# Gaps between SBUF tiles that set the distance, modulo 256 bytes, between the feed-forward tiles and the weights

## The chip, the cores and the metric

The kernel runs on one core of one Trainium2 chip. The metric is the device time of one execution in microseconds (us). One execution was also profiled; all rows below are of that one.

## What is computed

The reference has two stages. A gated linear attention runs over 4 batches, 8 heads, 768 positions and a head size of 48:

```
state = alpha[t] * state + outer(k[t], v[t])
y[t]  = q[t] @ state
```

Its output, 3072 tokens of width 384, goes through a feed-forward layer with 2048 hidden units:

```
h   = x @ w_in
g   = 0.5 * h * (1 + erf(h / sqrt(2)))
out = g @ w_out
```

Inputs and output are float32, the two weight matrices float64.

## The kernel before

**Feed-forward part.** The tokens are cut into 12 groups g of 256, the hidden units into 8 pieces f of 256. One (g, f) is a step, so there are 96 steps. To keep float32 precision, every operand of a matmul is split into a high and a low part of type float32r, and three products are added: high by high, high by low, low by high. `gemm1` (line 543) makes, for a step, 18 matmuls of 128 x 128 weights by 256 columns: the weights `wih` and `wil` are loaded as the stationary operand, the tile `x` streams through. Its result, the PSUM tile `hp`, is read twice by ScalarE (`gelus`, lines 555 and 556: GELU to the high half `ghi`, then GELU in place), and VectorE makes the low half `glo` from both (`gelu_low`, line 561). `gemm2` (line 582) makes 12 matmuls of 384 columns: here the halves `ghi` (8) and `glo` (4) are loaded as the stationary operand, and the weights `woh` and `wol` stream. So the weights are the loaded side in gemm1 and the streamed side in gemm2.

On TensorE each matmul is a pair, a weight load (PEld) and a matmul (PE). The load of the next pair begins when the matmul of this pair begins, so both read SBUF at the same time: one reads the next stationary operand, the other the streaming one.

**Order.** The attention units, the conversion of the weights (loaded as float64 and split on the chip) and the steps are put in order ahead of time by a planner in the kernel with costs (`COST`) and ranks; it writes out the order of TensorE, VectorE, ScalarE and SyncE by hand. Of the gemms it keeps gemm1 of step n+1 ahead of gemm2 of step n. From about 370 us on, TensorE runs nothing but steps.

**Where the tiles lie.** SBUF addresses are given per partition. Pools are laid side by side, and tiles in a pool in the order of their first use, each rounded up to 32 bytes. The pool `const` comes first and holds all weights; then `work`; then `ffn` with three x tiles, `z` (the rows of x that a DMA spreads), two `ghi` and two `glo`. At the other end of SBUF lies the pool `stage` for the conversion; when it is done, the pool `late` takes its room and holds one further x tile, for the groups 3, 7 and 11. Adding up the sizes gives:

| tiles | bytes each | address of the first | modulo 256 | distance to the weights, modulo 256 |
|---|---|---|---|---|
| wih, wil, woh, wol (32 tiles) | 3072 | 53,536 | 32 | 0 |
| x of groups 0-2, 4-6, 8-10 (3 tiles) | 6144 | 168,544 | 96 | +64 |
| z | 2048 | 186,976 | 96 | +64 |
| ghi, glo (2 each) | 2048 | 189,024 | 96 | +64 |
| late x of groups 3, 7, 11 | 6144 | 223,200 | 224 | +192 |

All these sizes, and the slices that one matmul reads (512, 1024 or 1536 bytes), are whole multiples of 256, so each tile keeps its distance throughout. The three x tiles go round by the order in which they come free; that gives groups 0, 5, 9 the first, 2, 6, 10 the second and 1, 4, 8 the third.

Names and lines that the change touches: `x_tiles` (line 487 on), `x_high`, `gelus`, `gelu_low` and `gelu_rest`, all of which ask a pool for tiles.

## Time and profile before

| | us |
|---|---|
| median of 3 runs (lowest, highest) | 515.25 (514.54, 515.87) |
| the profiled execution | 515.5 |
| its span, first to last instruction | 513.9 |
| PE busy in the span | 500.7 (97%) |
| DVE, ACT, POOL busy | 297.6, 219.6, 40.3 |

A row of a group of instructions has the line, the engine, the operation, the tiles (written <- read), the form and the count. A matmul's duration in the profile is longer than its distance to the next one, since matmuls overlap in the array; where two matmuls follow each other without a break, duration and distance differ by about 163 ns throughout (a duration of 281 ns goes with a distance of 118 ns), so that a duration that is 4 ns longer means a step that is 4 ns longer per matmul. In this kernel's rows both 32-bit types are written f32.

### The profile page before, as it was taken

The page shows a single profiled execution, that of the slowest core. Times are in us where ns is not written, and L with a number is a line of the kernel's source. Part 1 is how long each engine was busy: PE and PEld are TensorE (multiplying, and loading weights), DVE is VectorE, ACT ScalarE, POOL GpSimd, SP SyncE. Part 2 cuts the span into 40 slices and gives each one's busy share as a digit, 9 for nine tenths or more (in the row PEclk, how much of TensorE's full clock was granted, in tenths as well). Part 3 has the DMA queues.
Part 4 walks back from the last instruction along what each step waited for, and adds up shares of the span by engine and source line. Part 5 has one row for each costly group of instructions (what it writes and reads, how often), then busy time and mean ns, then how long its engine had stood idle before and what let it go on. Part 6 is the DMA issues. An engine that isn't in the chain of part 4 may idle for free.

```text
span 513.9 us, 13811 instructions
## 1 busy us (share of the span) xinstructions
PE 500.7 (97%) x5974; PEld 482.2 (94%) x5974; DVE 297.6 (58%) x579; ACT 219.6 (43%) x468; POOL 40.3 (8%) x60
## 2 busy tenths in 40 slices
PE   8898999999999999999999999999999999999995
PEld 8777999999999999999999999999999999999995
DVE  6999999999849966677685365252232211211211
ACT  2677765555444445355453343344332222222221
POOL 4100110100011111121111011010000000000000
PEclk9999999999999999999999999999999999999999
DMA  8967553531033422433231020010010000000001
GB/s 303 348 198 238 210 151 112 186 124 62 1 124 110 140 94 87 159 100 99 104 110 64 0 75 6 1 42 9 1 40 9 0 33 2 32 0 1 32 1 35
DMA packets 15250, 44.20 MB, mean 86 GB/s; under 512 B 2224, under 2 KB 5728, under 8 KB 15184
## 3 DMA queue, kind: packets, MB, share of 16 engines
q1 hardware_dynamic: 13520, 38.44, 22.7%
q0 software_dynamic: 1232, 4.33, 2.2%
q8 instruction: 49, 0.80, 0.7%
q10 hardware_dynamic: 432, 0.49, 0.3%
q14 instruction: 17, 0.14, 0.1%
HBM read 36.18 MB, written 4.72 MB: 80 GB/s over the span
## 4 chain that ended last, share of the span: by engine, by line
PE 94%; ACT 2%; ACTq 1%; issue 1%; DVE 0%; POOL 0%; DVEq 0%; POOLq 0%
PE acc L582 40%; PE hp L543 39%; PE s L308 4%; PE ybank L464 3%; PE ybank L381 3%; PE ybank L403 2%; PE warm L87 2%; ACTq L535 1%; PE spare L986 1%; PE ybank L349 1%; ACT junk L164 1%; PE ybank L521 0%; ACT L555 0%; ACT x L527 0%; ACT hp L556 0%
## 5 line engine op out<-in xcount | busy, mean ns | idle before, releaser
L543 PE MATMUL hp<-x,wih 128*128 128x256 f32 x1152 | 208.6, 281 | 0.0
L543 PEld LDWEIGHTS hp<-x,wih 128*128 128x128 f32 x1152 | 179.3, 188 | 1.8
L543 PE MATMUL hp<-x,wil 128*128 128x256 f32 x576 | 160.9, 279 | 0.0
L555 ACT ACTIVATE ghi<-hp 128x512 fp32r<-128x512 f32 x96 | 57.4, 598 | 212.5 <-PE hp L543 212.4
L561 DVE TENSOR_TENSOR glo<-hp,ghi 128x512 fp32r<-128x512 f32 x92 | 63.0, 685 | 145.4 <-ACT hp L556 145.2
L582 PE MATMUL acc<-woh,ghi 128*128 128x384 f32 x384 | 132.5, 345 | 0.0
L582 PE MATMUL acc<-wol,ghi 128*128 128x384 f32 x384 | 129.2, 336 | 0.0
L543 PEld LDWEIGHTS hp<-x,wil 128*128 128x128 f32 x576 | 108.0, 188 | 0.0
L582 PE MATMUL acc<-woh,glo 128*128 128x384 f32 x384 | 82.6, 336 | 0.0
L582 PEld LDWEIGHTS acc<-woh,ghi 128*128 128x128 f32 x384 | 72.0, 187 | 3.0
L582 PEld LDWEIGHTS acc<-wol,ghi 128*128 128x128 f32 x384 | 72.1, 188 | 0.0
L582 PEld LDWEIGHTS acc<-woh,glo 128*128 128x128 f32 x384 | 68.4, 188 | 0.0
L556 ACT ACTIVATE hp<-hp 128x512 f32<-128x512 f32 x96 | 56.9, 593 | 0.0
L272 DVE TENSOR_TENSOR_SCAN pp<-akq,top 128x256 f32<-128x256 f32 x48 | 31.3, 680 | 23.6 <-POOL qk L282 21.5
L287 DVE TENSOR_TENSOR_SCAN rp<-akq,rp,top 128x255 f32<-128x255 f32 x48 | 35.3, 763 | 0.7
L282 POOL TENSOR_TENSOR qk<-akq,pp 128x512 f32<-128x512 f32 x18 | 23.8, 1324 | 134.5 <-PE ybank L464 75.9
L607 POOL DMA_DIRECT2D out_dram<-part x11 | 8.4, 762 | 263.2 <-DVE part L601 191.9
L512 ACT CAST x<-ybank 64x256 fp32r<-64x256 f32 (+4 forms) x60 | 20.0, 333 | 10.9 <-PE ybank L464 8.4
L308 PE MATMUL s<-qk,akq 48*64 48x112 f32 x768 | 23.9, 261 | 0.5 <-PE ybank L349 0.2
L516 DVE TENSOR_TENSOR x<-ybank,x 64x256 fp32r<-64x256 f32 (+3 forms) x54 | 19.2, 355 | 8.5 <-ACT x L512 7.6
L317 ACT COPY kn<-s 128x384 f32<-128x384 f32 x24 | 11.5, 480 | 26.2 <-PE s L308 19.3
L464 PEld LDWEIGHTS ybank<-qk,states 48*48 48x48 f32 x704 | 14.6, 119 | 7.3 <-issue 2.8
(78 smaller groups left out, 412.2 us busy)
## 6 DMA issues: line engine op xcount, KB each, us to landing
akq<-in_akq_dram SPq DMA_DIRECT2D x22, 768.0 KB, 4.7
st<-in_moe_w_in_dram SPq DMA_DIRECT2D x8, 768.0 KB, 5.1
st<-in_moe_w_out_dram SPq DMA_DIRECT2D x8, 768.0 KB, 4.4
vn<-in_v_dram SPq DMA_DIRECT2D x12, 384.0 KB, 4.0
out_dram<-part POOLq DMA_DIRECT2D x11, 384.0 KB, 3.1
x<-z SPq DMA_DIRECT2D x63, 32.0 KB, 2.3
akq<-in_akq_dram SPq DMA_DIRECT2D x2, 512.0 KB, 6.1
akq<-in_akq_dram SPq DMA_DIRECT2D x2, 256.0 KB
```

The costliest lines, as they stand in the source:

```text
L272: nc.vector.tensor_tensor_scan(pp[:, i], at[:, i], top, MID, ALU.mult, ALU.min)
L282: eng.tensor_tensor(out=qs[:, :, :, :CS], in0=by_chunk(qt), in1=by_chunk(pp), op=ALU.mult)
L287: nc.vector.tensor_tensor_scan(rp[:, i, G - 2 :: -1], at[:, i, G - 1 : 0 : -1], top[:, 1:], rp[:, i, G - 1 :], ALU.mult, ALU.min)
L308: nc.tensor.matmul(d["s"][o, h, e : e + KW], lhsT=d["kt"][r, i, t], rhs=d["qs"][r, i, j], start=True, stop=True)
L464: ins = nc.tensor.matmul(ybank[o, b, t : t + CS], lhsT=states[u][j][r, i], rhs=d["qs"][r, i, j, :CS], start=False, stop=True, skip_group_c ...
L512: nc.scalar.copy(hi, y)
L516: nc.vector.tensor_tensor(out=lo, in0=y, in1=hi.bitcast(F32), op=ALU.subtract)
L543: nc.tensor.matmul(hp[:, j, :], lhsT=a[:, j, i * P : (i + 1) * P], rhs=x[:, i, :], start=(j == 0 and i == 0 and n == 0), stop=(i == NK - 1 ...
L555: nc.scalar.activation(ghi, hp, AF.Gelu)
L556: nc.scalar.activation(hp, hp, AF.Gelu)
L561: nc.vector.tensor_tensor(out=glo, in0=hp, in1=ghi.bitcast(F32), op=ALU.subtract)
L582: nc.tensor.matmul(acc[t], lhsT=a[:, j, t * C : (t + 1) * C], rhs=w[:, j, :], start=(first and j == 0 and k == 0 and w is wo_hi[f]), stop= ...
```

## The change

A helper `gap` asks the pool for a tile that nothing reads or writes; it takes up room and moves what comes after it. The tiles x, ghi and glo get a tag each, so that each has its own place, and gaps are put ahead of some of them. Going through the new order of the pool (gap 128, x0, z, x1, gap 64, ghi0, glo0, ghi1, gap 192, x2, gap 64, glo1) gives x and z at 224 modulo 256, and ghi and glo at 32. The late tile lies at 224 already. Distances to the weights after the change: all x +192, all halves 0. `HOME` writes down which group takes which x tile, the same as before; the halves go in turn, the same as before. No instruction is added, removed or moved to another place in the order.

```diff
--- before.py
+++ after.py
@@ -31,6 +31,8 @@
 LANES = 8
 RATE, ALONE, LATENCY, SMALL, BEGIN = 350e3, 290e3, 2.1, 50e3, 2.2
 MARGIN = 1.5
+HOME = {0: 0, 1: 1, 2: 2, 4: 1, 5: 0, 6: 2, 8: 1, 9: 0, 10: 2, "s": 1}
+X_GAP, Z_GAP, HI_GAP, LO_GAP, LATE_GAP = (128, 0, 192), 0, (64, 0), (0, 64), 0
 COST = dict(
     scan=0.65, back=0.72, keys=0.65, q=1.35, qv=0.62, scores=1.0, kn=0.5, mask=0.62, inside=1.05, chain=1.15, outer=0.85, carry=0.26, last=0.34, last_p=0.15, sums=0.55, scaled=0.45,
     xh=0.6, xl=0.65, spread=0.62, check=0.95, load=0.46, fetch=0.46, u=0.92, c0=0.56, c1=0.9, c2=0.45, c3=0.95, c4=0.92,
@@ -98,6 +100,10 @@
     top = column("top", TOP).to_broadcast([P, G])
     n_checks = NG * NPAIR // 2
     outside = const.tile([P, 2, n_checks], F32, name="outside")
+
+    def gap(pool, nbytes, name):
+        if nbytes:
+            pool.tile([P, nbytes // 4], F32, name=name, bufs=1)
 
     NB = 2
     vbuf = []
@@ -481,8 +487,12 @@
     def x_tiles(g):
         if g != "s" and g % (XB + 1) == XB:
             x = late[0].tile([P, NK, 2, G], F32R, tag="xl", name=f"x{g}")
+            if g == XB:
+                gap(late[0], LATE_GAP, "gap_late")
         else:
-            x = ffn.tile([P, NK, 2, G], F32R, tag="x", bufs=XB, name=f"x{g}")
+            if g in range(XB):
+                gap(ffn, X_GAP[HOME[g]], f"gap_x{g}")
+            x = ffn.tile([P, NK, 2, G], F32R, tag=f"x{HOME[g]}", bufs=1, name=f"x{g}")
         xt[g] = x[:, :, 0], x[:, :, 1]
         return x
 
@@ -507,6 +517,8 @@
         if u == 0:
             cur[g, "x"] = x_tiles(g)
         else:
+            if g == 0:
+                gap(ffn, Z_GAP, "gap_z")
             cur[g, "z"] = ffn.tile([P, 2, G], F32R, tag="z", bufs=1, name=f"z{g}")
         for y, hi, _ in x_parts(g, u):
             nc.scalar.copy(hi, y)
@@ -550,14 +562,23 @@
                     )
         return hp
 
+    halves = {}
+
+    def half_tile(what, gaps, g, f):
+        n = halves.get(what, 0)
+        halves[what] = n + 1
+        if n < 2:
+            gap(ffn, gaps[n], f"gap_{what}{n}")
+        return ffn.tile([P, 2, G], F32R, tag=f"{what}{n % 2}", bufs=1, name=f"{what}_{g}_{f}")
+
     def gelus(g, f, hp):
-        ghi = ffn.tile([P, 2, G], F32R, tag="ghi", name=f"ghi_{g}_{f}")
+        ghi = half_tile("ghi", HI_GAP, g, f)
         nc.scalar.activation(ghi, hp, AF.Gelu)
         nc.scalar.activation(hp, hp, AF.Gelu)
         return ghi
 
     def gelu_low(g, f, hp, ghi):
-        glo = ffn.tile([P, 2, G], F32R, tag="glo", name=f"glo_{g}_{f}")
+        glo = half_tile("glo", LO_GAP, g, f)
         nc.vector.tensor_tensor(out=glo, in0=hp, in1=ghi.bitcast(F32), op=ALU.subtract)
         return glo
 
@@ -565,7 +586,7 @@
         nc.tensor.matmul(hp, lhsT=minus, rhs=ghi, start=False, stop=True, skip_group_check=True)
 
         def out():
-            glo = ffn.tile([P, 2, G], F32R, tag="glo", name=f"glo_{g}_{f}")
+            glo = half_tile("glo", LO_GAP, g, f)
             nc.scalar.copy(glo, hp)
             return glo
```

## Rows read from the trace of the kernel before

**Rows 1.** page, busy time of each engine, and the chain that ended last
```profile
PE 500.7 (97%) x5974; PEld 482.2 (94%) x5974; DVE 297.6 (58%) x579; ACT 219.6 (43%) x468; POOL 40.3 (8%) x60
...
PE acc L582 40%; PE hp L543 39%; PE s L308 4%; PE ybank L464 3%; PE ybank L381 3%; PE ybank L403 2%; PE warm L87 2%; ACTq L535 1%; PE spare L986 1%; PE ybank L349 1%; ACT junk L164 1%; PE ybank L521 0%; ACT L555 0%; ACT x L527 0%; ACT hp L556 0%
```

**Rows 2.** windows: us, busy PE, PEld, DVE, ACT, POOL (x), PEclk, DMA share, GB/s
```profile
40.00:80.00 40.00, 38.53 (x582) 36.07 (x577) 38.90 (x69) 27.35 (x57) 2.82 (x3) 1.00 0.60 206
...
400.00:440.00 40.00, 40.00 (x286) 40.00 (x285) 7.87 (x12) 9.96 (x19) 0.72 (x1) 1.00 0.03 11
```

**Rows 3.** timeline: the GELU and the subtraction that follow one gemm1, ACT and DVE
```profile
449.77 0.60 ACT L555 ACTIVATE ghi<-hp 128x512 fp32r<-128x512 f32 x1 [3.15 <-PE hp L543]
...
450.89 0.69 DVE L561 TENSOR_TENSOR glo<-hp,ghi 128x512 fp32r<-128x512 f32 x1 [3.54 <-ACT hp L556]
```

**Rows 4.** windows of line 543 alone: us, busy PE, PEld (xinstructions), PEclk, DMA share, GB/s
```profile
80.00:159.30 79.30, 38.37 (x306) 37.28 (x304) 1.00 0.28 93
...
206.50:330.50 124.00, 54.77 (x432) 52.74 (x433) 1.00 0.23 72
330.50:369.20 38.70, 18.15 (x144) 17.57 (x145) 1.00 0.06 17
369.20:472.70 103.50, 54.64 (x432) 53.67 (x433) 1.00 0.04 14
```

**Rows 5.** timeline, PE: start, us: steps begin on x10 (first, second), on x11
```profile
439.01 0.39 PE L543 MATMUL hp<-x,wih 128*128 128x256 f32 x2
...
443.22 0.40 PE L543 MATMUL hp<-x,wih 128*128 128x256 f32 x2
...
472.80 0.39 PE L543 MATMUL hp<-x,wih 128*128 128x256 f32 x2
```

**Rows 6.** timeline, PE: start, us: the late tile x11, up to its last step
```profile
474.84 0.33 PE L582 MATMUL acc<-woh,ghi 128*128 128x384 f32 x1
...
476.92 0.40 PE L543 MATMUL hp<-x,wih 128*128 128x256 f32 x2
...
479.04 0.34 PE L582 MATMUL acc<-woh,ghi 128*128 128x384 f32 x1
...
502.15 0.40 PE L543 MATMUL hp<-x,wih 128*128 128x256 f32 x2
```

**Rows 7.** line 543, min/median/max ns: x10; its last; x11 first step; second; last
```profile
L543 PE MATMUL hp<-x,wih x12: 276/279/279, 439.0 to 440.9; 128*128 128x256 f32 x12
...
L543 PE MATMUL hp<-x,wil x1: 277/277/277, 441.0 to 441.0; 128*128 128x256 f32 x1
...
L543 PE MATMUL hp<-x,wih x11: 275/276/276, 472.8 to 474.5; 128*128 128x256 f32 x11
...
L543 PE MATMUL hp<-x,wih x12: 280/281/281, 476.9 to 478.8; 128*128 128x256 f32 x12
...
L543 PE MATMUL hp<-x,wil x1: 285/285/285, 478.9 to 478.9; 128*128 128x256 f32 x1
```

**Rows 8.** line 543 after a break of PE's stream: x3 (late), then x5 twice
```profile
L543 PE MATMUL hp<-x,wih x12: 276/276/383, 176.0 to 177.9; 128*128 128x256 f32 x12
...
L543 PE MATMUL hp<-x,wih x24: 276/276/384, 252.4 to 256.4; 128*128 128x256 f32 x24
...
L543 PE MATMUL hp<-x,wih x11: 278/279/384, 278.0 to 279.9; 128*128 128x256 f32 x11
```

**Rows 9.** line 582, min/median/max ns: x10, two steps in turn; x11
```profile
L582 PE MATMUL acc<-woh,ghi x4: 333/337/339, 441.1 to 442.2; 128*128 128x384 f32 x4
...
L582 PE MATMUL acc<-woh,ghi x3: 338/338/338, 445.7 to 446.4; 128*128 128x384 f32 x3
...
L582 PE MATMUL acc<-woh,ghi x3: 335/335/335, 479.4 to 480.1; 128*128 128x384 f32 x3
```

**Rows 10.** plain f32 matmuls, min/median/max ns: lines 87 and 365
```profile
L87 PE MATMUL warm<-ident x18: 274/275/275, 7.3 to 9.2; 128*128 128x128 f32 x18
...
L365 PE MATMUL ybank<-states,ident x2: 326/326/326, 26.5 to 26.7; 128*128 128x192 f32 x2
```

## The prediction, made before the result was known

> **What bounds the kernel now.** I read the page first: TensorE is busy in 97% of the span, and the chain that ended last runs through gemm2 (40%) and gemm1 (39%) [rows 1]. The reader should see there that only TensorE's own pace can matter. [...] Nothing else is close: the GELU waited 3.15 us for its gemm1, and the low half, begun at 450.89 and 0.69 us long, waited 3.54 us for ScalarE [rows 3]. So each nanosecond that a matmul is farther from the next one is paid in full, 18 times a step in gemm1 and 12 times in gemm2.

> Then the timeline, for the pace. The eight steps of group 10 lie between 439.01 and 472.80 us: 4.224 us a step [rows 5]. The late tile x11 holds the same work at another address: its last six steps begin from 476.92 to 502.15, 4.205 us each [rows 6]. And its first step took 472.80 to 476.92, 4.12 us: gemm1 2.04 us, 113.3 ns a matmul, where the second step's gemm1 (476.92 to 479.04) has 2.12 us, 117.8 ns [rows 5, 6]. The same matmuls thus run at two paces, and the durations mark them: 276 ns in the first step of x11, 281 in the second, 279 on x10 [rows 7]. In gemm2 there are 335 ns on x11, 338 in one step of x10 and a mix of 333 to 339 in the next [rows 9]. [...]

> **The change, part by part.** No instruction, wait or DMA is added or moved; HOME repeats the places that the x tiles take now, the halves go in turn as before, and a gap costs room alone. What changes is the distance between what streams and what is loaded, modulo 256 bytes.

> *gemm1 on the nine +64 groups goes to +192.* That is the late tile's case, so its price has rows. In an unbroken stream x11 mostly has 281 ns, where +64 has 279: no gain. After a break of TensorE's stream it differs: five gemm1 runs on late tiles came after one (first duration 383 ns or more, at 159.5, 176.0, 184.3, 336.0 and 340.9 us), and all five settled at 276 ns. On +64 tiles after 80 us there are eleven such runs, of which two did (at 149.4 and 252.4); the others stay at 279 [one of each, rows 8]. Nine runs with ten steps can change over: 10 x 18 x 4.4 ns (2.12 less 2.04 us, over 18) = 0.8 us.

> *gemm2, streaming weights, halves loaded: from distance 64 to 0.* No row has a whole gemm2 at 0. The nearest is its price on x11, 335 ns, against 338 and the mix on x10: the halves and weights have the same addresses in both, and only what gemm1 left behind differs. I take that, since gemm1 will be as on x11. With gemm1's small loss it is in the step times: 4.224 less 4.205 is 0.019 us. After 80 us, line 543 has 306, 432 and 432 matmuls on +64 tiles, 65 steps, and 3 x 144, 24 steps, on late ones [rows 4]; four of the 65 are the short ones at 149.4 and 252.4 us. 61 x 0.019 = 1.2 us. Bounds: below, the f32 matmuls of line 365, whose 192 columns stream as long as 384 of float32r (line 87's 128 columns have 275 ns, like 256 of gemm1), have 326 ns, 9 less than 335 [rows 9, 10]; above, the one distance that shows a loss. This is the last matmul of gemm1 on x11, which streams x at 224 while halves at 96 load: 285 ns against 281, 4 more [rows 7].

> *The seams.* The last gemm1 matmul of a late step goes from 285 back to 281: some 16 x 4 ns = 0.06 us. On the other tiles it loads halves at distance 0 now (277 ns against 279 [rows 7]) and at 192 after: at most 4 ns x 65 = 0.26 us lost or nothing; I take nothing, as +192 shows the pace of its tile. The seam from gemm2 to gemm1 stays at 0. z and the DMAs into x keep their sizes.

> Sum: 0.8 + 1.2 + 0.06 = 2.1 us off the profiled 515.5 us (span 513.9 and 1.6 around it), which lies 0.25 above the median of the runs; from the median, **513.2 us**. Both gains are off TensorE's path alone, so nothing takes their place: the halves are ready some 3 us early.

> [...]

> **Rivals.**

> *Short pace throughout.* With gemm2 at 0, gemm1 may be entered as in the first step of x11 and stay at 276 ns: 61 steps and the 16 late ones that are long now, 18 x 4.4 ns = 79 ns each, 6.1 us, and gemm2's 0.02 us in 65 steps, 1.3 us: 507.8. For it: 276 held through whole steps at both distances. Against: of the late tiles' steps that follow gemm2 without a break only two got there, and those behind a gemm2 of a +64 tile.

> *No change.* The paces follow from how a run is entered, both occur at +64 and at +192 [rows 7, 8], and the mix stays; or the gaps don't come out where they should. 515.2, give or take 1. [...]

> *Slower: gemm2 at distance 0.* What streams and what is loaded then begin in the same place modulo 256, twelve times a step. If this costs what +128 costs at the seam, 4 ns over the present 337 or so, then 89 steps x 12 x 4 = 4.3 us, less the 0.9 of the breaks and seams: 518.7. It decides from 0.9 us / 1068 = 0.8 ns a matmul on, measured from now: above 338 ns throughout it is slower. Against it: the seams at 0 show no loss today (277 against 279 [rows 7]).

> **How the numbers follow.** A difference under 0.3%, 1.5 us, can't be told from no change by a measurement of this kernel. Forecast, 511.5 to 514.5: 0.34, of which 0.27 beyond 1.5 us and 0.07 within. Short pace (and anything better, down to the bound of rows 10: 9 ns x 1068 = 9.6 us more): 0.23. No change: 0.19. Slower: 0.24. Together faster 0.50, same 0.26, slower 0.24. For 8 in 10 the range leaves out the best part of the short pace and the worst of the slower case: 506 to 519. The forecast's own range is 511.5 to 514.5.

> **What would show it.** Right: gemm1 on x10 at 281 in an unbroken stream and 276 after breaks, gemm2 at 335 on all tiles, steps of 4.205 us, no 285 at the seam. Short pace: 276 in most steps, 4.12 us. Wrong: gemm2 above 338, or below 333 (then distance 0 has a pace of its own), or any wait of TensorE that is not there now.

## The result, and the profile after

| | before | after |
|---|---|---|
| median of 5 runs, us (lowest, highest) | 514.99 (514.54, 515.87) | 509.92 (509.1, 510.61) |
| ratio of the times, 95% interval | | 0.9894 (0.9881 to 0.9907) |
| the profiled execution, its span, us | 515.5, 513.9 | 510.61, 509.0 |

By that ratio the change is faster by 1.06%, about 5.5 us; the two medians differ by 5.1 us, 0.98%, which is within the interval. The prediction said 513.2, in a range of 506 to 519. The forecast's own range was 511.5 to 514.5, and the measured time lies below it.

First the page of the changed kernel, the busy time of each engine. Lines have moved: gemm1 is line 555 now, gemm2 603.

```profile
PE 495.7 (97%) x5974; PEld 477.0 (94%) x5974; DVE 297.3 (58%) x579; ACT 219.6 (43%) x468; POOL 39.1 (8%) x60
```

TensorE's busy time fell by 5.0 us, about as much as the span; DVE and ACT have what they had [rows 1]. Where it went shows in the timeline of TensorE (start, duration; the first row of a step, and one of its gemm2's):

```profile
80.76 0.39 PE L555 MATMUL hp<-x,wih 128*128 128x256 f32 x2
...
435.53 0.39 PE L555 MATMUL hp<-x,wih 128*128 128x256 f32 x2
...
437.57 0.34 PE L603 MATMUL acc<-woh,ghi 128*128 128x384 f32 x1
...
468.55 0.39 PE L555 MATMUL hp<-x,wih 128*128 128x256 f32 x2
...
472.67 0.39 PE L555 MATMUL hp<-x,wih 128*128 128x256 f32 x2
...
497.43 0.39 PE L555 MATMUL hp<-x,wih 128*128 128x256 f32 x2
```

Eight steps on x10, 435.53 to 468.55, take 4.128 us each, where they took 4.224 [rows 5]; six on x11, 472.67 to 497.43, take 4.127, where they took 4.205 [rows 6]. In 435.53 to 437.57, gemm1 takes 2.04 us, the pace of x11's first step before. The durations (minimum, median, maximum) say the same, for gemm1 on x10, gemm1 on x11, gemm2, and a gemm1 behind a break:

```profile
L555 PE MATMUL hp<-x,wih x11: 275/276/276, 435.5 to 437.2; 128*128 128x256 f32 x11
...
L555 PE MATMUL hp<-x,wih x11: 275/276/276, 476.8 to 478.5; 128*128 128x256 f32 x11
...
L603 PE MATMUL acc<-woh,ghi x3: 334/334/334, 442.1 to 442.7; 128*128 128x384 f32 x3
...
L555 PE MATMUL hp<-x,wih x12: 281/281/384, 243.4 to 245.4; 128*128 128x256 f32 x12
```

gemm1 is at 276 ns on both tiles in the unbroken stream, against 279 and 281 [rows 7]; gemm2 at 334 once its first two matmuls (337 and 340 ns) are past, against 335 to 338 [rows 9]. But the run behind a break, at 243.4 us, has 281. Going through the timeline from 80 us on, run by run of gemm1: in the unbroken stream 5 of 72 had the short pace (276 ns) before, 70 of 73 have it now; behind a break 7 of 16 had it before, 5 of 16 now.

What stands ahead of a run sorts these counts. Directly behind a gemm2, 2 of 63 runs were short before, and all 64 are now. Nine unbroken runs follow another gemm1 instead, and each has the pace of the one ahead of it, before and after. The three long ones among the 73 are of that kind: the run ahead of each came behind a break and was long. Here is one of them, and the next run behind a gemm2:

```profile
L555 PE MATMUL hp<-x,wil x7: 281/281/281, 186.0 to 188.1; 128*128 128x256 f32 x7
...
L555 PE MATMUL hp<-x,wih x12: 275/276/276, 195.3 to 197.1; 128*128 128x256 f32 x12
```

These runs are the account. The step that began just short of 80 us in the kernel before is the one at 80.76 us above:

```profile
79.73 0.40 PE L543 MATMUL hp<-x,wih 128*128 128x256 f32 x2
```

From it to the last step, at 502.15 us [rows 6] and 497.43 us, the time fell from 422.42 to 416.67 us, by 5.75. gemm1 in the unbroken stream: 65 more runs x 79 ns = 5.1 us. Behind breaks, two fewer: 0.2 us lost. The rest, 0.8 us, is gemm2's. Adding up the times from each TensorE matmul's start to the next one's over this stretch says the same: gemm1 190.24 to 185.32 us, gemm2 189.45 to 188.62, everything else 42.73 in both. The profiled span gained only 4.9, since the changed kernel was 1.0 us late at this step. In its stretch of 48 to 50 us the granted clock of TensorE was 0.55 (the columns are us, busy us of PE, granted clock, DMA share, GB/s):

```profile
48.00:50.00 2.00, 2.00 (x12) 0.55 0.86 272
```

TensorE had stood idle for 1.2 us shortly ahead, up to 45.3 us. The experiment e12 below, idle for 1.35 us up to 45.9 us, kept 1.00 in the same stretch:

```profile
48.00:50.00 2.00, 2.00 (x29) 1.00 0.48 152
```

The executions of the changed kernel have a mean clock of 0.995 to 0.998, those of the kernel before, on the chips of the experiments, one of 0.992 to 0.999; the ranges overlap, and this is not counted as a part of the change.

### The profile page after: what moved, and what is told of

The parts are those of the page before. It is cut to its first block, busy times and chain, and to the rows that moved or that the text cites. A ratio compares the mean times of both kernels' runs of the same rounds, so it can differ in the third digit from the quotient of the medians.

```text
span 509.0 us, 13811 instructions
## 1 busy us (share of the span) xinstructions
PE 495.7 (97%) x5974; PEld 477.0 (94%) x5974; DVE 297.3 (58%) x579; ACT 219.6 (43%) x468; POOL 39.1 (8%) x60
## 4 chain that ended last, share of the span: by engine, by line
PE 80%; issue 12%; ACT 2%; DVE 2%; DMA 2%; POOL 1%; SPq 0%; ACTq 0%; DVEq 0%; POOLq 0%
PE acc L603 34%; PE hp L555 33%; PE s L314 3%; PE ybank L470 3%; PE ybank L387 2%; PE ybank L409 2%; DMA st<-in_moe_w_in_dram 2%; PE spare L1007 1%; ACT junk L170 1%; PE ybank L355 1%; POOL qk L288 1%; PE ybank L533 0%; ACTq L547 0%; SPq L158 0%; ACT L576 0%
## 5 line engine op out<-in xcount | busy, mean ns | idle before, releaser
L555 PE MATMUL hp<-x,wih 128*128 128x256 f32 x1152 | 204.7, 280 | 0.0
L314 PEld LDWEIGHTS s<-qk,akq 48*64 48x64 f32 x768 | 19.4, 133 | 3.8 <-issue 2.8
```

Source lines behind the costliest of these rows:

```text
L314: nc.tensor.matmul(d["s"][o, h, e : e + KW], lhsT=d["kt"][r, i, t], rhs=d["qs"][r, i, j], start=True, stop=True)
L555: nc.tensor.matmul(hp[:, j, :], lhsT=a[:, j, i * P : (i + 1) * P], rhs=x[:, i, :], start=(j == 0 and i == 0 and n == 0), stop=(i == NK - 1 ...
```

## The experiments

Each ratio compares with runs of the kernel before on the same chip; their medians were 515.64 us for e1 to e4, 515.21 for e5 to e8 and 515.22 for e9 to e12, so a time in the table is not to be held against 514.99. Each experiment but two changes only the gaps, in the one line of constants of the changed kernel; what matters are the distances that come out of it, which the table has. "Unbroken" and "behind a break" are counted as above, from 80 us on.

| run | x | ghi, glo | time, us | ratio (95%) | short gemm1, unbroken | behind a break | unbroken step, us |
|---|---|---|---|---|---|---|---|
| before | +64, late +192 | +64 | 514.99 | 1 | 5 of 72 | 7 of 16 | 4.224, 4.205 |
| changed kernel | +192 | 0 | 509.92 | 0.9894 (0.9881 to 0.9907) | 70 of 73 | 5 of 16 | 4.127 |
| e1 | +192 | +64 | 513.48 | 0.996 (0.995 to 0.9969) | 5 of 73 | 16 of 16 | 4.207 |
| e2 | +64 | 0 | 515.04 | 0.9994 (0.9982 to 1.0006) | 0 of 73 | 0 of 16 | 4.207 |
| e3 | +192 | +64, 0 | 508.64 | 0.9866 (0.9847 to 0.9885) | 70 of 73 | 6 of 16 | 4.120 |
| e4 | +192 | 0, +64 | 510.72 | 0.991 (0.9888 to 0.9932) | 69 of 72 | 5 of 16 | 4.140 |
| e5 | 0 | 0 | 516.85 | 1.0036 (1.0019 to 1.0053) | 0 of 72 | 0 of 16 | 4.233 |
| e6 | +128 | 0 | 517.13 | 1.0029 (1.0012 to 1.0046) | 0 of 73 | 0 of 16 | 4.227 |
| e7 | +192 | 0, all 256 further | 509.8 | 0.9893 (0.9871 to 0.9915) | 70 of 73 | 5 of 16 | 4.127 |
| e8 | +192 | +128 | 514.16 | 0.9982 (0.9969 to 0.9995) | 29 of 73 | 11 of 16 | 4.233 |
| e11 | +192 | +192, 0 | 511.25 | 0.9911 (0.9892 to 0.993) | 70 of 73 | 5 of 16 | 4.147 |
| e12 | as e3 | as e3 | 509.12 | 0.9875 (0.9855 to 0.9895) | 69 of 72 | 6 of 16 | 4.120 |

**Half of the change alone: e1 and e2.**

e1:

```diff
-X_GAP, Z_GAP, HI_GAP, LO_GAP, LATE_GAP = (128, 0, 192), 0, (64, 0), (0, 64), 0
+X_GAP, Z_GAP, HI_GAP, LO_GAP, LATE_GAP = (128, 0, 128), 0, (128, 0), (0, 128), 0
```

e2:

```diff
-X_GAP, Z_GAP, HI_GAP, LO_GAP, LATE_GAP = (128, 0, 192), 0, (64, 0), (0, 64), 0
+X_GAP, Z_GAP, HI_GAP, LO_GAP, LATE_GAP = (0, 0, 64), 0, (192, 0), (0, 192), 128
```

> All x at +192, GELU halves left at +64. Theory H (the seam hands over a phase: gemm1 at +192 is short only behind a gemm2 whose halves are at 0): gemm1 stays at 281 ns in an unbroken stream, as on the late tile of before, steps of about 4.205 us, 513.5 to 514.5 us. Theory O (each gemm's pace is set by its own distance alone): gemm1 at 276 ns, gemm2 as before at 336 to 338 ns, steps of about 4.15 us, 510.5 to 511.5 us.

> Halves at 0, all x (the late one too) at +64. Theory H: gemm1 can fall into either pace, since what enters it has changed; 276 ns would put it at 509 to 511 us, 279 to 281 at 513 to 515. Theory O: gemm1 279 ns as before on +64, gemm2 334 ns as after the change, 513 to 514 us.

e1, durations of gemm1 in the unbroken stream, of its last matmul, of gemm2, and of a gemm1 behind a break:

```profile
L555 PE MATMUL hp<-x,wih x11: 280/281/281, 412.9 to 414.7; 128*128 128x256 f32 x11
...
L555 PE MATMUL hp<-x,wil x1: 285/285/285, 414.9 to 414.9; 128*128 128x256 f32 x1
...
L603 PE MATMUL acc<-woh,ghi x3: 335/335/335, 415.4 to 416.1; 128*128 128x384 f32 x3
...
L555 PE MATMUL hp<-x,wih x11: 276/276/276, 244.3 to 246.0; 128*128 128x256 f32 x11
```

e2, gemm1 and gemm2 in the unbroken stream:

```profile
L555 PE MATMUL hp<-x,wih x11: 276/279/279, 414.3 to 416.1; 128*128 128x256 f32 x11
...
L603 PE MATMUL acc<-wol,ghi x4: 334/334/338, 416.6 to 417.7; 128*128 128x384 f32 x4
```

x alone is worth 0.4%, the halves alone (with the late tile brought to +64 as well) nothing that can be measured, both together 1.06%: more than the sum. With x at +192 and halves at +64 the whole kernel does what the late tile did before: 281 ns, a last matmul of 285, gemm2 at 335, steps of 4.207 us, and 276 behind each of the 16 breaks. Theory O is out: gemm1's own distance is the same in e1 and in the changed kernel, and its pace isn't. So what runs ahead of gemm1 decides: behind a gemm2 one run of 64 is short in e1, all 64 in the changed kernel. In e2 gemm2 did get shorter, by 0.55 us from the step near 80 us on, and gemm1 lost 0.47, in part on the late tile; its 515.04 us is at the edge of what theory H gave for 279 ns.

**Which part of gemm2: e3 and e4.** The eight loads of ghi come first in gemm2, the four of glo last.

e3:

```diff
-X_GAP, Z_GAP, HI_GAP, LO_GAP, LATE_GAP = (128, 0, 192), 0, (64, 0), (0, 64), 0
+X_GAP, Z_GAP, HI_GAP, LO_GAP, LATE_GAP = (128, 0, 128), 0, (128, 64), (192, 64), 0
```

e4:

```diff
-X_GAP, Z_GAP, HI_GAP, LO_GAP, LATE_GAP = (128, 0, 192), 0, (64, 0), (0, 64), 0
+X_GAP, Z_GAP, HI_GAP, LO_GAP, LATE_GAP = (128, 0, 192), 0, (64, 192), (64, 128), 0
```

> x at +192, ghi at +64, glo at 0: the last four loads of gemm2 are as after the change, the first eight as before. Theory H in the form that the last loads of gemm2 decide: gemm1 276 ns, gemm2 335, 509.5 to 511 us. If the first eight decide: gemm1 281, about 514. Theory O: gemm1 276 ns whatever the halves do.

> x at +192, ghi at 0, glo at +64: the mirror of the run before it. Theory H with the last loads deciding: gemm1 281 ns, 513 to 514.5 us. With the first eight deciding: gemm1 276 ns, 509.5 to 511. Theory O: gemm1 276 ns, 510 to 511.

e3, gemm1 and gemm2:

```profile
L555 PE MATMUL hp<-x,wih x12: 275/276/276, 414.7 to 416.6; 128*128 128x256 f32 x12
...
L603 PE MATMUL acc<-woh,ghi x3: 335/335/335, 417.1 to 417.8; 128*128 128x384 f32 x3
```

e4, gemm1, and the loads of glo in gemm2:

```profile
L555 PE MATMUL hp<-x,wih x12: 275/276/276, 414.5 to 416.4; 128*128 128x256 f32 x12
...
L603 PE MATMUL acc<-woh,glo x4: 334/338/338, 418.0 to 418.5; 128*128 128x384 f32 x4
```

Both have the short gemm1. Neither the first loads nor the last decide alone, and both forms of theory H fall that named one of them; either part at 0 was enough. e3's 508.64 us is below every range that was named for it. In e4 the change of distance inside gemm2 is paid there (338 against 334 ns, 13 ns a step over the changed kernel's 4.127).

**Other distances of x: e5 and e6, with halves at 0.**

e5:

```diff
-X_GAP, Z_GAP, HI_GAP, LO_GAP, LATE_GAP = (128, 0, 192), 0, (64, 0), (0, 64), 0
+X_GAP, Z_GAP, HI_GAP, LO_GAP, LATE_GAP = (192, 0, 0), 0, (0, 0), (0, 0), 192
```

e6:

```diff
-X_GAP, Z_GAP, HI_GAP, LO_GAP, LATE_GAP = (128, 0, 192), 0, (64, 0), (0, 64), 0
+X_GAP, Z_GAP, HI_GAP, LO_GAP, LATE_GAP = (64, 0, 128), 0, (128, 0), (0, 128), 64
```

> x and halves all at 0. Theory P (the pair of distances decides which of the two paces, 276 or 281 ns, gemm1 falls into in an unbroken stream): it can land on either; 509 to 511 us if short, 513.5 to 515.5 if long. Theory K (a distance of 0 is a collision of the two reads and costs by itself): gemm1 above 283 ns, over 517 us.

> x at +128, halves at 0. +128 is the distance at which the last gemm1 matmul of the late tiles took 285 ns before. Theory S (a distance has its own cost): gemm1 at about 285 ns throughout, 4 ns x 18 x 89 steps = 6 us more than before's pace, about 520 us. Theory P: one of the two paces again, 509 to 511 or 513.5 to 515.5 us.

gemm1 in e5, then in e6:

```profile
L555 PE MATMUL hp<-x,wil x5: 280/283/283, 414.6 to 416.1; 128*128 128x256 f32 x5
```

```profile
L555 PE MATMUL hp<-x,wil x5: 279/281/285, 416.2 to 417.6; 128*128 128x256 f32 x5
```

Theory P, which knew two paces, is wrong in both. In e5 the starts lie 120.0 ns apart for most of a run, a third pace, at the same clock; that is theory K's way, at a smaller price than its bounds (283 ns, 516.85 us); that the two reads collide isn't shown by it. In e6 they lie 118.9 apart on average, with single matmuls of 279 to 285; theory S wanted 285 throughout and 520 us. Both are slower than before by 0.3 to 0.4%. The granted clock was 1.00 in both, as it was before [rows 2]; here e5's windows row (granted clock, DMA share and GB/s last):

```profile
400.00:440.00 40.00, 40.00 (x283) 40.00 (x282) 7.87 (x12) 10.73 (x20) 0.73 (x1) 1.00 0.03 11
```

Of the four distances tried, multiples of 64, only x at +192 shows the short pace directly behind a gemm2; but it doesn't guarantee it. The distances 0 and +128 were tried with halves at 0 alone.

**The control: e7**, the first gap 256 bytes larger.

```diff
-X_GAP, Z_GAP, HI_GAP, LO_GAP, LATE_GAP = (128, 0, 192), 0, (64, 0), (0, 64), 0
+X_GAP, Z_GAP, HI_GAP, LO_GAP, LATE_GAP = (384, 0, 192), 0, (64, 0), (0, 64), 0
```

> The changed kernel with 256 bytes more ahead of all x and halves, so that every distance is the same modulo 256 and every tile lies elsewhere. If only the distance modulo 256 matters: gemm1 276 ns, gemm2 334, steps of 4.127 us, within 0.3% of the changed kernel (509 to 511 us). If the place itself matters: any other.

```profile
L555 PE MATMUL hp<-x,wih x11: 276/276/276, 414.9 to 416.6; 128*128 128x256 f32 x11
```

The same paces, the same counts, the same time. For this one shift, modulo 256 is enough to describe the address. The weights stayed where they were in every run, and here the late tile did too. So whether the distance to the weights counts, or the place of x and the halves by itself, isn't shown.

**Both paces at one address: e8.**

```diff
-X_GAP, Z_GAP, HI_GAP, LO_GAP, LATE_GAP = (128, 0, 192), 0, (64, 0), (0, 64), 0
+X_GAP, Z_GAP, HI_GAP, LO_GAP, LATE_GAP = (128, 0, 64), 0, (192, 0), (0, 192), 0
```

> x at +192, halves at +128. Theory P: a further entry into gemm1, 276 or 281 ns; 509 to 511 or 513.5 to 515.5 us. If only halves at 0 let gemm1 be short: 281 ns, about 514.

gemm1 of group 7 at 330 us, and of group 9 at 413 us, both in the unbroken stream:

```profile
L555 PE MATMUL hp<-x,wih x10: 276/276/276, 330.0 to 331.6; 128*128 128x256 f32 x10
...
L555 PE MATMUL hp<-x,wih x12: 279/281/281, 412.8 to 414.7; 128*128 128x256 f32 x12
```

Up to 370 us 29 of 43 unbroken runs are short; from 381 us on all 30 are long, with the same distances. In e8 the pace mostly passes through gemm2: where gemm1, gemm2 and gemm1 follow without a break, 18 of 18 runs behind a short one are short, and 29 of 33 behind a long one long. In e1 and in the changed kernel it does not: gemm2 turns 7 of 7 short ones into long ones in e1, and 5 of 5 long ones into short ones in the changed kernel.

Every change from short to long in e8 lies at a break, directly ahead of gemm1 or ahead of the gemm2 before it: of the 13 runs behind a gemm2 that began behind a break, 10 are long. At the last such change the attention's matmuls come between two gemm2, and no further break follows:

```profile
378.26 0.67 PE L470 MATMUL ybank<-qk,states 48*48 48x64 f32 x32
378.86 0.44 PE L603 MATMUL acc<-woh,ghi 128*128 128x384 f32 x1
...
381.07 0.40 PE L555 MATMUL hp<-x,wih 128*128 128x256 f32 x2
```

Why such a break goes with the long pace in 10 cases and not in three wasn't found.

**Moving the entry: e9 and e10.** One more matmul of 32 columns goes ahead of gemm1's first one; the first one overwrites what it wrote. e9 has the distances of e1, e10 those of the changed kernel.

```diff
         hp = ps_h.tile([P, 2, G], F32, tag="hp", name=f"hp_{g}_{f}")
+        nc.tensor.matmul(hp[:, 0, :32], lhsT=wi_hi[f][:, 0, :P], rhs=xhi[:, 0, :32], start=True, stop=True, skip_group_check=True)
         for j in range(2):
```

> The kernel with x at +192 and halves at +64 (281 ns in an unbroken stream), with one more matmul of 32 columns ahead of gemm1's first, into the same PSUM columns, which the first then overwrites. Addresses are the same, only the moment at which gemm1's stream begins moves. It costs up to one load, 113 ns a step, 10 us in all. Entry theory (the moment of entry picks the pace): gemm1 may change over to 276 ns, about 517 us; a switch in most unbroken steps would show it. Address theory (the pair of distances fixes the pace): 281 ns as without it, about 523.5 us.

> The same further matmul in the changed kernel (276 ns in an unbroken stream). Entry theory: gemm1 may lose its short pace, 281 ns, about 525 us, or keep it if the shift is the same as none. Address theory: 276 ns as without it, about 519.5 us.

e9, timeline of one entry:

```profile
404.82 0.18 PE L552 MATMUL hp<-x,wih 128*128 128x32 f32 x1
...
404.85 0.48 PE L556 MATMUL hp<-x,wih 128*128 128x256 f32 x2
```

e9, the durations of that gemm1 after its first matmuls, then e10's:

```profile
L556 PE MATMUL hp<-x,wih x8: 276/276/276, 405.6 to 406.8; 128*128 128x256 f32 x8
```

```profile
L556 PE MATMUL hp<-x,wih x10: 276/276/276, 404.8 to 406.3; 128*128 128x256 f32 x10
```

In e9, 60 of the 63 unbroken runs that have the further matmul close behind gemm2 are short, against 1 of 64 behind gemm2 in e1, at the same addresses. The matmul behind the first real one starts 201 ns after it, much as behind a break (some 220 ns), and four matmuls later the run is at 276. So the pair of distances doesn't fix the pace, and the address theory is out for this pair.

That the moment of entry picks it is not shown. The further matmul also changes what stands directly ahead of gemm1, and the same 201 ns stands in the nine runs that follow another gemm1, which are all long, even behind a short one as here:

```profile
L556 PE MATMUL hp<-x,wih x9: 281/281/281, 188.0 to 189.4; 128*128 128x256 f32 x9
```

Behind a break 12 of 16 are short, where e1 has 16 of 16. e10 stays short in 64 of 64 behind gemm2, which both theories allowed; behind another gemm1 three of nine are short, behind a break 10 of 16. The times were 520.17 and 519.53 us, one run each: the further matmul costs more than it brings (e9's steps take 4.247 us against 4.207). e9 came out 3 us over what was expected. In all it has 51 more short runs than e1, worth 4.0 us, where the expectation counted 6.5; that is most of it.

**A better pair: e11 and e12.**

e11:

```diff
-X_GAP, Z_GAP, HI_GAP, LO_GAP, LATE_GAP = (128, 0, 192), 0, (64, 0), (0, 64), 0
+X_GAP, Z_GAP, HI_GAP, LO_GAP, LATE_GAP = (128, 0, 0), 0, (0, 192), (64, 64), 0
```

e12:

```diff
-X_GAP, Z_GAP, HI_GAP, LO_GAP, LATE_GAP = (128, 0, 192), 0, (64, 0), (0, 64), 0
+X_GAP, Z_GAP, HI_GAP, LO_GAP, LATE_GAP = (128, 0, 128), 0, (128, 64), (192, 64), 0
```

> x at +192, ghi at +192, glo at 0. If glo at 0 is enough for the short pace whatever ghi does: gemm1 276 ns, 508 to 511 us. If it takes a matching ghi too (0 or +64): 281 ns, 513 to 515 us.

> The best pair so far once more, x at +192, ghi at +64, glo at 0, in more rounds: 276 and 335 ns, steps of 4.120 us against the changed kernel's 4.127. From the steps it should be some 0.6 us below the changed kernel, 0.986 to 0.989 of the time before. If its lead in the earlier set was chance: 0.989 as the changed kernel.

e11, the loads of glo in gemm2:

```profile
L603 PE MATMUL acc<-woh,glo x4: 334/340/346, 415.2 to 415.7; 128*128 128x384 f32 x4
```

In e11 gemm1 is short with ghi at +192 too (its 511.25 us is just above the 508 to 511 named for that), and gemm2 pays with up to 346 ns where ghi gives way to glo. e12, e3 once more, has the shortest steps of all, 4.120 us, and was ahead of the changed kernel in both sets; but the intervals of 0.9866 and 0.9875 overlap with that of 0.9894, and 7 ns x 89 steps are 0.6 us, so the lead over the changed kernel is not shown. Against before it is: 1.2 to 1.3%.

## Why the prediction was right or wrong

**Right: what bounds, and where the time would come from.** TensorE's pace was all that moved; no wait took the place of what was saved (TensorE's time outside the two gemms, from the step near 80 us on, is 42.73 us before and after), and the paces that occurred in the trace before, 276 and 281, 334 to 338, are the ones that the changed kernel has. The sign and the wide range held. The size did not come from the sum: 509.92 lies outside the forecast's own range of 511.5 to 514.5, and the wide range covers it because it left room for the rival with the short pace, which had a chance of 0.23.

**Mis-sized: "In an unbroken stream x11 mostly has 281 ns ... no gain", and gemm2's "I take that, since gemm1 will be as on x11".** The forecast took gemm1 on the moved tiles to be what it was on x11, while the halves in front of it were moved as well. e1 is that assumption in pure form: 513.48 us against 515.64 before, 2.2 us less where the sum had 2.1, and 4.207 us a step where it had 4.205. Moving the halves turned gemm1 to the short pace in 70 of 73 unbroken runs; that is 5.1 us in the unbroken stream, which the sum had at nothing. That is the rival "short pace throughout" (507.8 us); its mechanism came, but not behind breaks and not quite everywhere, hence 509.9. Its condition, gemm1 entered as in the first step of x11, was on the row: that step followed a gemm2 of another pace. The long and the short gemm1 on x11 [rows 7] had the address in common and not the entry. The prediction saw this and put it among the rivals; its sum went by the commoner of the two paces.

**Wrong: 0.8 us behind breaks.** All five late runs had the short pace there, and e1 keeps it in 16 of 16. With the halves at 0, eleven of 16 are long. Five rows were good evidence for halves at +64 and none for halves at 0. The term came out at 0.2 us lost.

**Near in size, but not owed to distance 0: gemm2.** 334 ns in the steady part of gemm2, against 335 taken, and 0.8 us in all where the sum had 1.2. It doesn't take distance 0: e1, with the halves left at +64, has 188.16 us of gemm2 in the stretch from the step near 80 us on, 1.3 less than before, and the changed kernel 188.62. So the move of x alone brings it, and with the halves at 0 and a short gemm1 ahead gemm2 takes some 0.5 us more than that. The slower rival needed a larger cost there; with x at +64, e2's gemm2 is 0.55 us shorter than before, and its time is the same (0.9994). That rival's cost does show on x: at 0 and at +128 gemm1 is slower (e5, e6).

**The seam.** The sum took 285 ns as the last gemm1 matmul of some 16 late steps. In the trace before nine have it, so the term was 0.04 us instead of 0.06.

**The place of x.** In e2, e5, e6 and the changed kernel gemm2's halves are at the same distance, the granted clock is 1.00 in the unbroken stream and the instructions are the same; gemm1 lies between 113.3 and 120.0 ns a matmul behind gemm2, and only the place of x differs. That a load and the stream beside it meet in SBUF, no run here shows: in the trace before, a load begins 2 to 4 ns ahead of the matmul beside it (284 loads, 400 to 440 us), but no weights were moved, and no load was taken away from beside its stream. The shortest steady distances of any run are 113.3 ns in gemm1 and 173.3 ns in gemm2 (steps of 4.120 us, of which gemm1 takes 2.04).

**Open.** What in a gemm2 sets the pace of the gemm1 behind it, why the same breaks give opposite paces with halves at +64 and at 0, and why a break ahead of gemm2 goes with the long pace in e8 in some cases only. Distances off multiples of 64 were not tried, nor moved weights.

## What to carry to other kernels

Where TensorE is the bound and streams and loads from SBUF without a break, compare the start to start of equal matmuls across the run: here two paces of the same instruction, 117.8 and 113.3 ns, were 5.1 us to be had without touching an instruction. Try the distances of all operands together, modulo 256 bytes: here x alone was worth 0.4%, the halves alone nothing that can be measured, both 1.06%. A single tile that already lay elsewhere told its own pace only under the neighbours that it had: at one and the same address x11 had 281 ns before the change and 276 after it. Don't forecast from steady rows alone: look at how the run with the better pace was entered.
